# Fixing where sixteen weight tiles are converted: a data tie to a head's maxima and another order of the three integer steps

## The chip, the cores and the metric

The kernel runs on one core of a Trainium2 chip. The metric is the device time of one execution in microseconds (us). Engines are called by the names of the profile: PE (TensorE), DVE (VectorE), ACT (ScalarE), POOL (GpSimd), SP (SyncE, which only issues DMAs here).

## The reference

Block-causal attention over 8 batches of 8 heads (576 positions, head width 64), then a gated feed-forward layer over the 4608 tokens:

```python
scores = scale * np.matmul(q, k.transpose(0, 1, 3, 2))
scores = np.where(mask, scores, -1000000000.0)          # mask: block_i >= block_j, blocks of 64
scores = scores - np.max(scores, axis=-1, keepdims=True)
attn = np.exp(scores)
attn = attn / (np.sum(attn, axis=-1, keepdims=True) + 1e-09)
x = np.matmul(attn, v)                                   # then heads side by side: (4608, 512)
h = x @ w_in                                             # (4608, 2048)
sp = np.maximum(h, 0.0) + np.log1p(np.exp(-np.abs(h)))
out = (h * erf(sp)) @ w_out                              # (4608, 512)
```

The attention inputs are float32, the weights float64 (handed over as pairs of 32-bit words), the output float32.

## The kernel before, in words

**The heads.** A Python loop over n = 0 to 66 (line 663) lays out 64 heads as a software pipeline. In round n it emits the load of head n+3 (line 394: two POOL-issued DMAs into one of four buffers `qk0` to `qk3`, one SP-issued DMA into `st`), the row maxima of head n+2 (`maxes`, line 405: PE scores at L412, DVE reductions at L415 into the tile `mx0` or `mx1`, by the parity of n; L440, a PE transpose at L442, an ACT copy `mt` at L444 and a small DMA put them into the head's `qk` buffer), the probabilities of head n (`probs`: PE at L458 and L459, ACT exponentials at L463), and for every second n the product with v of the two heads before (`pv`: PE at L507 and, for the sums, L530). `normalise` (line 559) follows for each four heads: reciprocals at L570, their split into `r2` at L571 and L572 on DVE, a PE transpose `ru` at L582, scaling at L592, and the store to `x_d`.

**The weights.** 16 tiles in two halves each, so 32 conversions from float64 to float32. A conversion's 512 KB (`raw`, two buffers, line 112) is loaded by SP (L115). `to_f32` (line 118) makes a float32 from the two words of each float64: an ACT step (L122) writes `a` from the high word, and three DVE steps (L123, L124, L125) put the float32 together in `t`. L123 takes the low word alone, L124 and L125 read `a`. A last ACT step (L128) sums the squares. `a` lies in the tag `r0`, three buffers that the gate of the feed-forward layer uses too. The table `TOF` (line 641) says in which rounds conversions are emitted: one in rounds 0 and 1, two in rounds 2 to 8 and 11 to 18. In rounds 9 and 20 `scale_group` (line 545) turns the sums of squares of a group of eight tiles into a scale, and `split_w` (line 143) makes float16 pairs.

**The feed-forward layer.** From round 10 on `moe1` (line 271) puts pieces of it between the attention's (`up` at L193, `gate` at L161 to L169, `down` at L202), as far as attention has finished tokens and tiles of weights are split. What is left runs after the loop, in the code from line 714 on.

**What sets the order.** `merge` (line 217) interleaves the pieces of a round by fractions of the round. This is the program's order; a scheduler then decides in what order each engine gets its instructions. It lets an instruction go ahead of earlier ones where nothing that it reads or writes holds it back, so a conversion can be put into an engine's queue ahead of the round that emitted it. Each engine works through its queue in that order and stands still when the next instruction has to wait.

The functions that the diff touches, and their callers:

Of the kernel before, what the change touches and what calls it, by code (L numbers as in the profile page):

```python
# [14 lines left out]
ALU = mybir.AluOpType  # L15
# [8 lines left out]
def f32(ap):  # L24
    return ap.bitcast(F32)


def i32(ap):
    return ap.bitcast(I32)
# [3 lines left out]
def tile_attention_moe(ctx: ExitStack, tc: tile.TileContext, qk, v, w, maskrows, selws, out):  # L33
    nc = tc.nc
# [66 lines left out]
    def raw_t(f):  # L101
        return f32(slots[f + 1].rearrange("p a b -> p (a b)"))
# [12 lines left out]
        nc.sync.dma_start(raw, w[f, s].bitcast(I32))  # L115
        return raw.rearrange("p (n t) -> p n t", t=2)

    def to_f32(f, s, raw):

        t = i32(raw_t(f)[:, s * DM : (s + 1) * DM])  # L120
        a = mpool.tile([P, DM], F32, tag="r0", name=f"a{f}_{s}")
        nc.scalar.activation(a, f32(raw[:, :, 1]), AF.Copy, scale=2.0**-112)  # L122
        nc.vector.tensor_scalar(out=t, in0=raw[:, :, 0], scalar1=29, scalar2=None, op0=ALU.logical_shift_right)  # L123
        nc.vector.scalar_tensor_tensor(out=t, in0=i32(a), scalar=3, in1=t, op0=ALU.logical_shift_left, op1=ALU.bitwise_or)  # L124
        nc.vector.scalar_tensor_tensor(out=t, in0=i32(a), scalar=-0x80000000, in1=t, op0=ALU.bitwise_and, op1=ALU.bitwise_or)  # L125
        g = group[f]
        j = f - GROUPS[g][0]
        nc.scalar.activation(a, f32(t), AF.Square, accum_out=wss[g][:, s, j : j + 1])  # L128
# [169 lines left out]
    with tc.tile_pool(name="apool", bufs=2) as apool, tc.tile_pool(name="spool", bufs=1) as spool, \  # L298
# [6 lines left out]
        mxs = [spool.tile([P, 7], F32, name=f"mx{i}") for i in range(2)]  # L305
# [83 lines left out]
        def load_qk(n):  # L389
            b, h = divmod(n, H)  # L390
            t = qks[n % NB][:, : 4 * S].rearrange("p (i n) -> p i n", n=S)
            st = apool.tile([P, S], F32, tag="st", name=f"st_{n}", bufs=2)

            def a():
                nc.gpsimd.dma_start(t[:D, 1:4, :], qk[b, h, D:].rearrange("(s d) n -> d s n", d=D))
                nc.sync.dma_start(st, qk[b, h, : 2 * D])
                nc.gpsimd.dma_start(t[D:, 0:2, :], qk[b, h, : 2 * D].rearrange("(s d) n -> d s n", d=D))

            def c():
                nc.gpsimd.tensor_tensor(out=t[:D, 0, :], in0=st[:D, :], in1=f32(t[:D, 2, :]), op=ALU.subtract)  # L400
                nc.gpsimd.tensor_tensor(out=t[D:, 1, :], in0=st[D:, :], in1=f32(t[D:, 1, :]), op=ALU.subtract)  # L401

            return a, c
# [147 lines left out]
        def scale_b(b):  # L551
            vsb = vs[b * NQ + NQ - 1][0]
            nc.vector.tensor_copy(binv[b], vsb[:, 1:2])
            for g in range(2):
                if scaled[g]:
                    scale_bg(b, g)
            known.append(b)
# [57 lines left out]
        raws = {}  # L615

        def next_raw(src=None):
            if len(raws) < len(HALVES):
                fs = HALVES[len(raws)]
                raws[fs] = load_raw(*fs, apool, src)  # L620
# [9 lines left out]
        def late(kind, steps):  # L630

            def run(f):
                tc.cur_priority += PRIO.get(kind, 0)
                f()
                tc.cur_priority -= PRIO.get(kind, 0)
            return [lambda f=f: run(f) for f in steps]
# [4 lines left out]
        TOF = {0: 1, 1: 1, 2: 2, 3: 2, 4: 2, 5: 2, 6: 2, 7: 2, 8: 2} | {n: 2 for n in range(11, 19)}  # L641
        SCALE_AT = {9: 0, 20: 1}
        SPLIT = {9: 2, 10: 3, 11: 3, 20: 2, 21: 2, 22: 2, 23: 2}
        def conv():
            fs = HALVES[len(conved)]
            conved.append(fs)
            if len(raws) < len(conved):
                next_raw()
            to_f32(*fs, raws[fs])
            if len(raws) == len(conved):  # L650
                next_raw()

# [10 lines left out]
        for n in range(N + 3):  # L663
            lists = []
            if n + NB - 1 < N:
                load, low = load_qk(n + NB - 1)
                lists += [(late("load", [load]), 0, LQ), (late("low", [low]), LQ, 1)]
            if n + 2 < N:
                *steps, rows[n + 2] = maxes(n + 2)
                lists.append((late("max", steps), 0, 1))  # L670
            if n + 1 in rows:
                lists.append((late("max", [rows.pop(n + 1)]), 0, 0.6))
            if n < N:
                prs[n] = []
                lists.append((late("prob", probs(n, prs[n])), 0, 1))
            qd = n // 4 + 1
            if n < 2:
                lists.append(([lambda v0=v32: scale_v(0, 0, *v0), lambda v0=v32: vs.__setitem__(0, prep_v(0, 0, *v0))][n : n + 1], 0.6, 0.8))
            if n % 4 == 1 and qd < N // 4:
                v32 = load_v(*divmod(qd, NQ), mxs[(n + 1) % 2][:1, 3:4])  # L680
            if n % 4 == 2 and qd < N // 4:
                lists.append((late("v", [lambda qd=qd: scale_v(*divmod(qd, NQ), *v32)]), 0, 1))
            if n % 4 == 3 and qd < N // 4:
                lists.append((late("v", [lambda qd=qd: vs.__setitem__(qd, prep_v(*divmod(qd, NQ), *v32))]), 0, 1))
            if n % 2 == 0 and 2 <= n <= N:
                j = n // 2 - 1
                qd, pp = divmod(j, 2)
                usbs[j] = apool.tile([P, S], F32, tag="usb", name=f"usb{j}", bufs=2)
                steps = pv(qd, pp, [prs.pop(2 * j), prs.pop(2 * j + 1)], vs[qd], usbs[j], rss[j % 2])
                lists.append((late("pv", steps), 0, 1))  # L690
                if pp == 1:
                    normals[n + 1] = qd
            if n in normals:
                qd = normals.pop(n)
                b, q_ = divmod(qd, NQ)
                lists.append((late("norm", normalise(b, q_, [usbs.pop(2 * qd), usbs.pop(2 * qd + 1)], rss)), 0.2, 0.8))
                if q_ == NQ - 1:
                    lists.append((late("norm", [lambda b=b: scale_b(b)]), 0, 0.2))
                    ready_at[n + 1] = (b + 1) * S // T
            ready = ready_at.get(n, ready)  # L700
            for _ in range(TOF.get(n, 0)):
                lists.append((late("conv", [conv]), 0, 1))
            if n == 2:
                lists.append(([selects], 0.5, 0.6))
            if n in SCALE_AT:
                lists.append(([lambda n=n: scale_group(SCALE_AT[n])], 0, 0.1))
            if n in SPLIT:
                lists.append((late("conv", [split_next] * SPLIT[n]), 0.1, 1))
            if n < 2:
                lists.append(([warm] * WARM, 0, 1))  # L710
            lists.append((late("moe", [lambda: moe1(ready)] * RATE[0 if n < 10 else 1 if n < 20 else 2]), 0, 1))
            merge(*lists)
# [49 lines left out]
```

## Time and profile before

| | |
|---|---|
| time, median of 3 runs | 1243.53 us (1240.6 to 1246.77) |
| the profiled execution's own time | 1237.53 us |
| its span in the profile | 1235.7 us |
| PE busy (matmuls) | 1147.4 us, 93% of the span |
| DVE busy | 811.4 us, 66% |
| ACT busy | 850.0 us, 69% |
| POOL busy | 479.1 us, 39% |
| read from and written to HBM | 121.69 MB and 28.31 MB |

The shares are means over a span whose parts differ. PE is close to full from about 300 us on. The conversions all lie in the first 240 us, where PE has idle time and where its granted clock is below full at times; so the numbers of the stretch count, not those of the span. The profiled execution took 6.0 us less than the median of the runs.

### The profile page before, as it was taken

Reading aid. Unit: us, or ns where it says so; the run is one execution under the profiler, and the core shown is the slowest. Engines: PE = TensorE matmul, PEld = TensorE weight load, DVE = VectorE, ACT = ScalarE, POOL = GpSimd, SP = SyncE. Lnnn points to the kernel's source line nnn. Section 1 sums busy time; section 2 is a strip of 40 time slices with the busy share of each in tenths; the row PEclk is TensorE's granted clock in tenths of the full one; section 3 lists DMA queues with packets and bytes.
Section 4 is the critical chain, followed back from the end, with each engine's and each line's share of the span. In section 5 each row is a group of like instructions: output and inputs, shape, how many; then the busy total and the mean of one; then the engine's idle time right before and its main releaser. Section 6 shows DMA issues by size and latency. Waiting matters only on the chain.

```text
span 1235.7 us, 23041 instructions
## 1 busy us (share of the span) xinstructions
PE 1147.4 (93%) x8874; PEld 794.2 (64%) x8874; DVE 811.4 (66%) x1535; ACT 850.0 (69%) x1651; POOL 479.1 (39%) x459
## 2 busy tenths in 40 slices
PE   6787988899999999999999999999989999999997
PEld 3454655566676667767676676776766766666663
DVE  4677797787567767677668666666667644554554
ACT  2465767587677767777777676677767776766664
POOL 6454455436443444535453444435444312100000
PEclk9787899999999999999999999999999999999999
DMA  9987667644545445444454444444444221221202
GB/s 234 246 214 191 164 186 184 189 114 121 119 130 135 113 108 136 131 134 111 115 138 101 121 117 126 110 124 114 120 114 114 57 64 56 68 68 52 69 27 77
DMA packets 95628, 151.73 MB, mean 123 GB/s; under 512 B 7611, under 2 KB 44795, under 8 KB 95519
## 3 DMA queue, kind: packets, MB, share of 16 engines
q1 hardware_dynamic: 69696, 93.34, 24.8%
q0 software_dynamic: 25152, 56.69, 21.6%
q8 instruction: 70, 1.15, 0.4%
q10 hardware_dynamic: 670, 0.23, 0.1%
q14 instruction: 40, 0.32, 0.1%
HBM read 121.69 MB, written 28.31 MB: 121 GB/s over the span
## 4 chain that ended last, share of the span: by engine, by line
PE 37%; ACT 25%; DVE 24%; DMA 7%; issue 5%; POOL 1%; ACTq 0%; DVEq 0%; SPq 0%; POOLq 0%
PE m_h L193 11%; PE o L202 11%; DVE m_r L165 6%; DVE m_r L166 5%; PE u L507 5%; DVE m_r L167 5%; ACT m_r L162 4%; ACT m_r L161 4%; ACT m_r L164 4%; ACT m_r L163 4%; DMA raw<-w 3%; ACT m_gh L168 2%; PE s L412 2%; PE t L458 2%; PE t L459 2%
## 5 line engine op out<-in xcount | busy, mean ns | idle before, releaser
L193 PE MATMUL m_h<-xh,w 128*128 128x256 f16 x2304 | 470.8, 274 | 14.5 <-DVE m_r L167 14.1
L193 PEld LDWEIGHTS <-w 128*128 128x128 f16 x3456 | 326.3, 98 | 146.7 <-issue 19.3
L202 PE MATMUL o<-w,m_gh 128*128 128x512 f16 x1152 | 334.2, 382 | 6.2 <-ACT m_gh L168 5.2
L193 PE MATMUL m_h<-xl,w 128*128 128x256 f16 x1152 | 314.9, 273 | 0.0
L415 DVE TENSOR_REDUCE mx<-s 64x1 f32<-64x288 f32 (+4 forms) x384 | 174.1, 468 | 108.7 <-PE s L412 107.9
L169 POOL TENSOR_TENSOR m_gl<-m_r,m_gh 128x512 f16<-128x512 f32 x114 | 136.6, 1199 | 272.5 <-ACT m_gh L168 244.9
L165 DVE SCALAR_TENSOR_TENSOR m_r<-m_r,m_r 128x512 f32<-128x512 f32 x144 | 116.6, 809 | 167.3 <-ACT m_r L164 161.9
L168 ACT CAST m_gh<-m_r 128x512 f16<-128x512 f32 x144 | 88.8, 617 | 176.6 <-DVE m_r L167 175.3
L202 PE MATMUL o<-w,m_gl 128*128 128x512 f16 x576 | 204.2, 385 | 0.0
L463 ACT ACTIVATE p<-t 128x288 f32<-128x288 f32 (+4 forms) x384 | 144.6, 384 | 74.4 <-PE t L459 64.1
L412 PE MATMUL s<-qk 68*64 68x288 f32 (+3 forms) x384 | 149.0, 421 | 28.7 <-DMA qk<-qk 22.2
L458 PE MATMUL t<-qk 69*128 69x288 f32 (+4 forms) x384 | 168.0, 438 | 7.4 <-DMA qk<-mt 3.7
L161 ACT ACTIVATE m_r<-m_h,c,bs 128x512 f32<-128x512 f32 (+3 forms) x192 | 124.1, 666 | 26.1 <-PE m_h L193 23.4
L202 PEld LDWEIGHTS <-m_gh 128*128 128x128 f16 x1152 | 100.7, 98 | 63.0 <-issue 8.5
L400 POOL TENSOR_TENSOR qk<-st,qk 64x576 fp32r<-64x576 f32 x64 | 94.7, 1479 | 116.1 <-DMA qk<-qk 112.6
L475 DVE TENSOR_TENSOR p<-p,p 128x832 f16<-128x832 f32 x80 | 81.5, 1018 | 63.6 <-ACT p L474 63.4
L459 PE MATMUL t<-qk 128*128 128x288 f32 (+4 forms) x384 | 120.5, 314 | 0.0
L166 DVE SCALAR_TENSOR_TENSOR m_r<-m_r 128x512 f32<-128x512 f32 x144 | 116.6, 810 | 3.2
L401 POOL TENSOR_TENSOR qk<-st,qk 64x576 fp32r<-64x576 f32 x64 | 97.3, 1520 | 34.5 <-DMA qk<-qk 30.8
L163 ACT ACTIVATE m_r<-m_r,c 128x512 f32<-128x512 f32 x144 | 103.7, 720 | 2.8 <-ACT m_r L162 0.7
L162 ACT ACTIVATE m_r<-m_r,c 128x512 f32<-128x512 f32 x144 | 103.7, 720 | 2.0
L164 ACT ACTIVATE m_r<-m_r,c 128x512 f32<-128x512 f32 x144 | 103.6, 719 | 2.1 <-ACT m_r L163 0.3
(108 smaller groups left out, 1432.4 us busy)
## 6 DMA issues: line engine op xcount, KB each, us to landing
qk<-qk POOLq DMA_DIRECT2D x64, 432.0 KB, 4.8
st<-qk SPq DMA_DIRECT2D x64, 288.0 KB
qk<-qk POOLq DMA_DIRECT2D x64, 288.0 KB, 4.9
raw<-w SPq DMA_DIRECT2D x32, 512.0 KB
v<-v SPq DMA_DIRECT2D x16, 640.0 KB
x_d<-xs POOLq DMA_DIRECT2D x32, 288.0 KB, 3.2
xh<-x_d SPq DMA_DIRECT2D x36, 256.0 KB
xl<-x_d SPq DMA_DIRECT2D x36, 256.0 KB
```

The costliest lines, as they stand in the source:

```text
L161: nc.scalar.activation(r0s[:, :, lo:hi], h[:, :, lo:hi], AF.Tanh, bias=const(p1), scale=bss[b][g][:, 0:1])
L162: nc.scalar.activation(r1, r0, AF.Square, bias=const(b1), scale=a1)
L163: nc.scalar.activation(r0, r1, AF.Square, bias=const(b2), scale=a2)
L164: nc.scalar.activation(r0, r0, AF.Square, bias=const(b3), scale=a3)
L165: nc.vector.scalar_tensor_tensor(out=r0, in0=r0, scalar=c4, in1=r1, op0=ALU.add, op1=ALU.mult)
L166: nc.vector.scalar_tensor_tensor(out=r0, in0=r0, scalar=c5, in1=r0, op0=ALU.add, op1=ALU.mult)
L193: nc.tensor.matmul(h[:, k, :], lhsT=wf[:, a, sl], rhs=x[:, cc, :], start=cc == 0 and i == 0, stop=cc == NCC - 1 and i == 2)
L202: nc.tensor.matmul(o[c], lhsT=a[:, sl], rhs=wf[:, b_, :], start=u == u0 and k == 0 and not lo and b_ == 2, stop=u == u1 - 1 and k == nu - ...
L412: nc.tensor.matmul(dst[:r, :w_], lhsT=qh[:K, i * P : i * P + r], rhs=kh[:K, k0 : k0 + w_], start=True, stop=True)
L415: nc.vector.tensor_reduce(out=mx[:r, col : col + 1], in_=src, axis=AX.X, op=ALU.max, negate=True)
L458: nc.tensor.matmul(s[:kk, :w_], lhsT=kh[:K, ks], rhs=qh[:K, q0 : q0 + w_], start=True, stop=False)
L459: nc.tensor.matmul(s[:kk, :w_], lhsT=klh[:, ks], rhs=qhl[:, q0 : q0 + w_], start=False, stop=True)
```

## The change

`to_f32` gets a fourth argument, a pointer to one element of a maxima tile, and a tiny DVE copy writes this element into the first element of `a` before the ACT step. The ACT step overwrites all of `a`, so no result changes; but it must now come after the copy, and the copy after the DVE reductions that wrote the element. `conv` passes on the argument: for the first conversion of round n column 0, for the second column 3 of `mx0` or `mx1`, which in that round belong to head n+2. And the DVE steps swap roles: the first shifts `a` left by 3, the second shifts the low word right by 29 and joins it, the third adds the sign as before. So no DVE step can run ahead of the ACT step any more, and the last reader of `raw` is the second DVE step, where it was the ACT step or the first DVE step.

```diff
-    def to_f32(f, s, raw):
+    def to_f32(f, s, raw, src):
 
         t = i32(raw_t(f)[:, s * DM : (s + 1) * DM])
         a = mpool.tile([P, DM], F32, tag="r0", name=f"a{f}_{s}")
+        nc.vector.tensor_copy(a[:1, :1], src)
         nc.scalar.activation(a, f32(raw[:, :, 1]), AF.Copy, scale=2.0**-112)
-        nc.vector.tensor_scalar(out=t, in0=raw[:, :, 0], scalar1=29, scalar2=None, op0=ALU.logical_shift_right)
-        nc.vector.scalar_tensor_tensor(out=t, in0=i32(a), scalar=3, in1=t, op0=ALU.logical_shift_left, op1=ALU.bitwise_or)
+        nc.vector.tensor_scalar(out=t, in0=i32(a), scalar1=3, scalar2=None, op0=ALU.logical_shift_left)
+        nc.vector.scalar_tensor_tensor(out=t, in0=raw[:, :, 0], scalar=29, in1=t, op0=ALU.logical_shift_right, op1=ALU.bitwise_or)
         nc.vector.scalar_tensor_tensor(out=t, in0=i32(a), scalar=-0x80000000, in1=t, op0=ALU.bitwise_and, op1=ALU.bitwise_or)
...
-        def conv():
+        def conv(src):
...
-            to_f32(*fs, raws[fs])
+            to_f32(*fs, raws[fs], src)
...
-            for _ in range(TOF.get(n, 0)):
-                lists.append((late("conv", [conv]), 0, 1))
+            for i in range(TOF.get(n, 0)):
+                lists.append((late("conv", [lambda src=mxs[n % 2][:1, 3 * i : 3 * i + 1]: conv(src)]), 0, 1))
```

From line 121 on the changed kernel's lines are one higher: the ACT step is L123 there, the DVE steps L124 to L126, the copy L121 plus one, L122.

The scheduler's order changes with it. The first place is DVE's queue in round 9, where the reciprocals of the second group of heads are split into `r2` (the PE transpose `ru` waits for it). `we0` and `wsb0` are the scale of the first weight group, `vm1_1` the maxima of a v tile, `raw8_1` the load of a conversion that round 11 emits. Before:

```order
L139 TENSOR_SCALAR we0_1137<-we0_1137 128x2
L348 TENSOR_REDUCE vm1_1_1352<-v1_1_1126 128x1
L140 TENSOR_SCALAR we0_1137<-we0_1137 128x2
...
L571 CAST r2_146<-ri0_1_1163 128x3x8
L123 TENSOR_SCALAR w9_101<-raw8_1_1519 128x512
L543 TENSOR_TENSOR bs0_0_113<-bs0_0_113,wsb0_111 128x1
L572 TENSOR_TENSOR r2_146<-ri0_1_1163,r2_146 128x3x8
```

Now:

```order
L140 TENSOR_SCALAR we0_1153<-we0_1153 128x2
L416 TENSOR_REDUCE mx1_150<-s01_11_1166 128x1
L141 TENSOR_SCALAR we0_1153<-we0_1153 128x2
...
L572 CAST r2_146<-ri0_1_1179 128x3x8
L542 SCALAR_TENSOR_TENSOR bs0_0_113<-bi0_159,wsb0_111 128x1
L543 SCALAR_TENSOR_TENSOR bs0_0_113<-bi0_159,wsb0_111 128x1
L573 TENSOR_TENSOR r2_146<-ri0_1_1179,r2_146 128x3x8
```

The step on `raw8_1` is gone from in front of the last instruction on `r2`, and the reduction `vm1_1` comes one round later.

The second place is ACT's queue in round 3, with the two conversions of tile 2 (`a2_0`, `a2_1`) between the exponentials of head 3 (`p0_3`, `p1_3`) and the copy of head 4's maxima (`mt_4`). Before:

```order
L122 ACTIVATE a2_1_578<-raw2_1_576 128x512
L463 ACTIVATE p0_3_532<-t0_3_0_537 128x288
L463 ACTIVATE p0_3_532<-t0_3_288_546 128x288
L444 CAST mt_4_556<-mt4_554 5x128
L463 ACTIVATE p0_3_532<-t3_3_320_559 128x192
L445 DMA qk0_129<-mt_4_556 1x5x128
L463 ACTIVATE p0_3_532<-t4_3_320_588 64x64
L463 ACTIVATE p1_3_533<-t1_3_128_595 128x448
L463 ACTIVATE p1_3_533<-t2_3_256_602 128x320
L122 ACTIVATE a3_0_660<-raw3_0_584 128x512
```

Now:

```order
L464 ACTIVATE p0_3_536<-t4_3_320_594 64x64
L445 CAST mt_4_560<-mt4_558 5x128
L446 DMA qk0_129<-mt_4_560 1x5x128
L123 ACTIVATE a2_0_574<-raw2_0_491 128x512
L123 ACTIVATE a2_1_583<-raw2_1_581 128x512
L464 ACTIVATE p1_3_537<-t1_3_128_601 128x448
L464 ACTIVATE p1_3_537<-t2_3_256_608 128x320
L464 ACTIVATE p0_4_613<-t0_4_0_619 128x288
```

The ACT steps of tile 2 come later, right behind one another and behind `mt_4`, and that of tile 3, which stood at the end of this piece, is now in the next round.

The third place is DVE's queue in round 4, the steps of tile 3's two halves (their result is in `w4`) among head 6's maxima. Before:

```order
L123 TENSOR_SCALAR w4_96<-raw3_0_584 128x512
L123 TENSOR_SCALAR w4_96<-raw3_1_666 128x512
L124 SCALAR_TENSOR_TENSOR w4_96<-a3_0_660,w4_96 128x512
L124 SCALAR_TENSOR_TENSOR w4_96<-a3_1_668,w4_96 128x512
L415 TENSOR_REDUCE mx0_149<-s2_6_644 128x1
L125 SCALAR_TENSOR_TENSOR w4_96<-a3_0_660,w4_96 128x512
L415 TENSOR_REDUCE mx0_149<-s3_6_657 128x1
L125 SCALAR_TENSOR_TENSOR w4_96<-a3_1_668,w4_96 128x512
L415 TENSOR_REDUCE mx0_149<-s4_6_0_682 64x1
```

Now:

```order
L122 COPY a3_0_666<-mx0_149 1x1
L126 SCALAR_TENSOR_TENSOR w3_95<-a2_1_583,w3_95 128x512
L416 TENSOR_REDUCE mx0_149<-s2_6_650 128x1
L416 TENSOR_REDUCE mx0_149<-s3_6_663 128x1
L124 TENSOR_SCALAR w4_96<-a3_0_666 128x512
L122 COPY a3_1_675<-mx0_149 1x1
L416 TENSOR_REDUCE mx0_149<-s4_6_0_690 64x1
L125 SCALAR_TENSOR_TENSOR w4_96<-raw3_0_590,w4_96 128x512
L124 TENSOR_SCALAR w4_96<-a3_1_675 128x512
L126 SCALAR_TENSOR_TENSOR w4_96<-a3_0_666,w4_96 128x512
L125 SCALAR_TENSOR_TENSOR w4_96<-raw3_1_673,w4_96 128x512
```

Two of the maxima reductions go ahead of the conversion, and `raw` is read by the second of the three steps, where it was read by the first.

## Rows read from the trace of the kernel before

**Rows 1.** Busy time by stretch; per engine us (count), then granted clock, DMA share, GB/s
```profile
25.00:105.00 80.00, 62.44 (x422) 40.62 (x421) 56.78 (x132) 43.60 (x124) 37.18 (x36) 0.81 0.93 228
115.00:125.00 10.00, 9.93 (x40) 6.64 (x40) 8.79 (x15) 6.97 (x14) 8.02 (x9) 0.50 0.39 104
125.00:250.00 125.00, 112.27 (x828) 75.70 (x825) 96.00 (x191) 85.00 (x195) 58.42 (x52) 0.93 0.68 182
300.00:1236.00 936.00, 900.95 (x7194) 630.28 (x7189) 590.78 (x1061) 666.29 (x1226) 327.65 (x298) 1.00 0.38 103
```

**Rows 2.** The page's list of DMA issues: KB each, median us to landing
```profile
qk<-qk POOLq DMA_DIRECT2D x64, 432.0 KB, 4.8
st<-qk SPq DMA_DIRECT2D x64, 288.0 KB
qk<-qk POOLq DMA_DIRECT2D x64, 288.0 KB, 4.9
raw<-w SPq DMA_DIRECT2D x32, 512.0 KB
```

**Rows 3.** The copies of maxima, one a head, 25 to 110 us: ns, first and last start
```profile
L444 ACT CAST mt<-mt x10: 238/255/257, 24.9 to 108.9; 5x128 fp32r<-5x128 f32 x10
```

**Rows 4.** Who waited for whom, 20 to 250 us: total, times, longest
```profile
ACT a L122 <- DMA raw<-w: 13.2, 4, 6.6
...
PE ru L582 <- DVE r L572: 8.6, 3, 5.0
...
DVE w L123 <- DMA raw<-w: 6.6, 5, 2.0
```

**Rows 5.** The chain of waits, 0 to 300 us: the loads of raw on it
```profile
67.21 8.01 DMA raw<-w
...
104.43 9.03 DMA raw<-w
...
181.90 6.44 DMA raw<-w
...
207.89 7.59 DMA raw<-w
```

**Rows 6.** DVE in order of time, round 9: start, us, in brackets the idle time before
```profile
108.22 0.20 DVE L139 TENSOR_SCALAR we<-we 128x2 int32<-128x2 int32 x1
109.48 1.49 DVE L348 TENSOR_REDUCE vm<-v 128x1 f32<-128x1280 f32 x1 [1.06 <-DMA v<-v]
...
113.48 0.43 DVE L123 TENSOR_SCALAR w<-raw 128x512 int32<-128x512 int32 x1 [1.28 <-DMA raw<-w]
...
113.89 0.18 DVE L572 TENSOR_TENSOR r<-ri,r 128x24 fp32r<-128x24 f32 x1
```

**Rows 7.** PE in order of time: round 9, and one later piece like the third row
```profile
108.88 0.28 PE L459 MATMUL t<-qk 128*128 128x256 f32 x1
114.22 0.80 PE L582 MATMUL ru<-ident,r 128*16 128x128 f32 x3 [5.05 <-DVE r L572]
...
120.74 5.50 PE L507 MATMUL u<-p,v 128*64 128x256 f32 x28
...
205.40 3.07 PE L507 MATMUL u<-p,v 128*64 128x256 f32 x28
```

**Rows 8.** PE in order of time: the longer waits for DVE after 125 us
```profile
159.78 0.49 PE L412 MATMUL s<-qk 68*64 68x288 f32 x1 [2.23 <-DVE mx L415]
...
172.81 0.49 PE L582 MATMUL ru<-ident,r 128*16 128x128 f32 x3 [1.47 <-DVE r L572]
...
190.17 0.47 PE L458 MATMUL t<-qk 69*128 69x448 f32 x1 [1.70 <-DVE mx L415]
...
226.76 0.49 PE L582 MATMUL ru<-ident,r 128*16 128x128 f32 x3 [2.13 <-DVE r L572]
```

**Rows 9.** Durations by line, ns least/median/most, first and last start
```profile
L122 ACT ACTIVATE a<-raw x32: 648/669/737, 23.3 to 229.6; 128x512 f32<-128x512 f32 x32
L123 DVE TENSOR_SCALAR w<-raw x32: 363/417/1632, 23.5 to 235.6; 128x512 int32<-128x512 int32 x32
L124 DVE SCALAR_TENSOR_TENSOR w<-a,w x32: 627/680/2672, 25.3 to 236.5; 128x512 int32<-128x512 int32 x32
L337 DVE COPY v<-mx x16: 131/142/143, 10.7 to 895.1; 1x1 f32<-1x1 f32 x16
```

## The prediction

> **What bounds the kernel now.** I read the table of busy time by stretch first [rows 1]. From 300 us on PE has matmuls in 901 of 936 us at full clock: that part is PE's own work, the change has no instruction in it, and whatever is won or lost before is carried to the end as a shift. The conversions lie between 23 and 238 us, where PE is busy 62 of 80 us and 112 of 125 us and its mean granted clock is 0.81 and 0.93 (levels 1.2 and 2.4 GHz). So the sum is over waits of PE in those stretches.
>
> Second, the loads. Up to 105 us DMA moves 228 GB/s at a busy share of 0.93 [rows 1]. A head needs 432 + 288 + 288 KB, and the two conversions of a round 2 x 512 KB [rows 2]: 2032 KB, 2.08 MB, at 228 GB/s 9.1 us. The copies of maxima come once a head: ten from 24.9 to 108.9 us, 9.3 us apart [rows 3]. So in rounds 2 to 8 bytes set the pace, and an engine that waits less gains little there. After 125 us DMA runs at 182 GB/s, and PE with its waits for other engines sets the pace.
>
> Third, who waits for raw. ACT waits four times, 13.2 us in all, of which the longest (6.6 us) is the start-up; DVE five times, 6.6 us [rows 4]. Both queues are in order, so what stands behind waits along. The chain of waits runs through four loads of raw, of 6.4 to 9.0 us [rows 5]; the one issued at 104.43 us is that of raw8_1, which landed at 113.46 us. Its reader on DVE is the step at 113.48 us [rows 6], two instructions ahead of the last one on r2, and PE's transposes of r2 started at 114.22 us after 5.05 us of nothing [rows 7]. This is PE's longest wait in the stretch, and the conversion that caused part of it was only needed two rounds later.
>
> **The change part by part.**
>
> *Round 9.* The order shows the raw step gone from ahead of r2's last instruction, and the reduction vm1_1 moved a round on. On DVE this takes out a wait of 1.06 and a work of 1.49 us for vm1_1, and a wait of 1.28 and a work of 0.43 us for raw8_1 [rows 6], 4.26 us of the 5.47 between the end of L139 (108.42) and the start of L572 (113.89). What remains are small steps that have their inputs. L572 then starts near 109.6 us and PE goes on at about 110.0 in place of 114.22. I take -4.2 us; the ends are -5.05 (PE never waits) and 0 (another late input, such as the maxima reductions put in there).
>
> *The clock behind it.* In the stretch 115 to 125 us the granted clock was 0.50, the 1.2 GHz level, with PE busy 9.93 of 10 us [rows 1]; PE had stood still for the 5.05 us before. The 28 matmuls with v took 5.50 us there and 3.07 us at full clock later [rows 7]. If the wait shrinks to about 1 us I expect the clock to stay up for these: -2.4 us. Ends: 0 (it falls anyway) and -5.0 (the whole stretch at double speed).
>
> *After 125 us.* Four longer waits of PE for DVE add up to 7.5 us [rows 8]. In front of r2 at 172.8 us a third conversion step is replaced by the small copy, and ahead of the maxima that PE waits for at 190.2 us a step on raw12_1 is gone; ahead of the other two the order keeps as much work. So -1.47 - 1.70 = -3.2 us; ends 0 and -7.5.
>
> *The copies.* 32 copies of one element, 0.142 us each by the nearest row, the same kind of copy for v [rows 9]: 4.5 us on DVE, which is busy 71 to 77% in these stretches [rows 1]. Only those in front of something PE waits for count: I take +1.0, ends 0 and +4.5.
>
> *The swapped steps.* The first step is again one that reads one tensor, and the second again one that reads two, both 128x512: 417 and 680 ns as before [rows 9], cost 0. What differs is that the first now reads a contiguous tile and the second a strided one; no row shows that pair, and I take the ends as plus and minus 32 x 0.1 us, mostly hidden.
>
> *The release of raw.* There are two raw buffers and, in most rounds, two conversions, so each buffer turns over once a round. Before, SP could issue the next load when the ACT step (0.67 us) and the first DVE step had read it. Now it must wait for ACT, then the first DVE step and the second: at least 0.42 + 0.68 = 1.1 us later [rows 9], more where DVE has maxima in between, as the order shows for tile 3. Who waits behind: ACT's queue, with the exponentials that free PE's banks behind the conversion. Nine of 32 loads were waited for already [rows 4]. In the first 105 us bytes set the pace and I count nothing; for two of the places later I count 1.1 us each: +2.2. Ends: 0, and the second rival's price.
>
> The Trainium skill's page "DMA: Bandwidth & Descriptors", in its section "Rules for kernel authors", says to issue a DMA early, compute, and wait for its semaphore late, and this change issues each load of weights later. By that rule the term would be the second rival's price in full; by the rows it is small, since the loads before 105 us take their time from bytes and not from when they are asked for.
>
> *Sum.* -4.2 - 2.4 - 3.2 + 1.0 + 2.2 = -6.6 us. The profiled execution took 1237.53 us (span 1235.7), so it would take 1230.9; it stands 6.0 us below the median of the runs, 1243.53, so I forecast 1237 us for a median. That is 0.53% less, hardly over the 0.5% that a measurement of this kernel can tell from no change.
>
> **The rivals.**
>
> *Little is left (within 0.5%).* The gain of round 9 comes, but the rounds before give it back: rounds 2 to 8 convert half a round later, and the 16 loads that must be there by round 9 are the same. If 4 us of the 6.6 of round 9 are lost to later loads and the waits after 125 us only change their names, -2.6 + 1 = about -2: 1241.5 us. For it speaks that bytes set the pace of that stretch, so a later start of loads is time of DMA not used; against it, that the head's own loads then come sooner. Into this case goes that the change does not do what it says: a tie to maxima that are there already holds nothing back. The order speaks against that, since the ACT steps did move.
>
> *The raw buffers become the bound (slower).* The place is ACT's queue in rounds 2 to 8. A turn of the two buffers is then a load (8.0 us for the one at 67 us [rows 5]), two ACT steps of 0.67 and two pairs of DVE steps of 1.1 us [rows 9]: 11.5 us, against 9.3 us a head. In seven rounds that is +15 us. With round 9's -6.6 and the copies' +1 the sum is +9.8, or 1253 us. It decides from the point where a load takes more than 9.3 - 3.5 = 5.8 us. For it speaks that all four loads on the chain took more than that; against it, that they took so long beside each other and beside the heads' loads, and that with fewer in flight each is shorter.
>
> **How the numbers follow.** The forecast (faster by over 0.5%, though the likeliest value is close to that bound) gets 0.41: the excerpt of round 9 is plain, and its price is read from one wait. The first rival gets 0.35. The second gets 0.24: the later release is certain, its cover is not. The range takes in the larger ends of round 9, the clock and the later waits (-5.05 - 5.0 - 5 + 1 = about -14, or 1229) and the second rival (1253); about 1 in 10 is left out on each side: 1229 to 1254. The forecast's own range is 1229 to 1241. Chances: faster 0.41, within 0.5% 0.35, slower 0.24.
>
> **What would show it.** Right: PE's wait ahead of ru in round 9 is about 1 us, the granted clock there stays near 1; no DVE step of a conversion waits for a DMA; PE's waits for r2 add up to less than 8.6 us; the tenth copy of maxima stands no later than 109 us. The second rival would show as ACT waiting for raw in most rounds from 3 to 8, far over 13.2 us in all, and the tenth copy of maxima at 115 us or later. I am wrong if the shift at 300 us differs from that at the end by over 3 us (then something in the last part changed), or if the gain comes from another place than round 9.

## The result, and the profile after

The changed kernel took **1255.65 us** (median of 4 runs, 1251.7 to 1259.34), the kernel before 1242.07 (median of 4): a ratio of 1.0127, 95% interval 1.0082 to 1.0172. It is slower by 1.3%, where 0.5% faster was forecast, and lies just above the range, 1229 to 1254 us. The profiled execution took 1256.76 us (span 1255.0).

Busy time by stretch of the changed kernel, in the columns of [rows 1], with three short stretches more:

```profile
25.00:105.00 80.00, 61.51 (x410) 40.57 (x408) 55.33 (x140) 42.99 (x118) 38.76 (x36) 0.79 0.91 219
115.00:125.00 10.00, 9.69 (x47) 6.18 (x45) 7.59 (x15) 6.91 (x15) 8.92 (x8) 0.62 0.48 109
125.00:250.00 125.00, 105.29 (x758) 68.66 (x759) 100.67 (x207) 80.97 (x186) 59.79 (x53) 0.93 0.64 171
...
206.00:212.00 6.00, 6.00 (x32) 3.12 (x32) 1.74 (x5) 3.59 (x9) 2.19 (x2) 0.56 1.13 337
240.00:250.00 10.00, 4.97 (x49) 3.12 (x48) 5.28 (x21) 4.94 (x13) 5.03 (x4) 0.94 0.45 129
250.00:260.00 10.00, 6.33 (x33) 4.54 (x33) 0.69 (x1) 0.73 (x3) 2.79 (x2) 0.54 0.95 215
300.00:1236.00 936.00, 906.81 (x7239) 636.38 (x7237) 594.66 (x1065) 668.90 (x1234) 333.17 (x305) 0.99 0.39 103
```

The three short stretches in the kernel before:

```profile
206.00:212.00 6.00, 6.00 (x51) 3.83 (x48) 5.87 (x9) 4.18 (x12) 1.41 (x1) 1.00 1.14 282
240.00:250.00 10.00, 10.00 (x101) 8.27 (x101) 2.52 (x12) 6.38 (x14) 3.31 (x4) 1.00 0.95 235
250.00:260.00 10.00, 8.28 (x60) 6.08 (x59) 9.79 (x26) 7.88 (x17) 7.03 (x7) 1.00 0.53 131
```

The stretch up to 105 us is as it was. Between 240 and 260 us PE was busy 11.3 us in place of 18.3, and from 250 us on mostly at the 1.2 GHz level (0.54). The copies of maxima (`mt_n`, one a head, as in [rows 3], where mt_10 is the tenth) date this exactly. Worked out from their starts in the two traces, and from a second execution of the changed kernel (run e8 below), in us:

```
                    0 to mt_10  mt_10-16  mt_16-19  mt_19-22  mt_22 to end
before                 108.9      90.4      38.3      45.9      952.2
changed                110.9      85.4      42.4      59.5      956.7
changed, once more     112.1      83.4      41.0      56.3      954.6
```

So the changed kernel takes 5 to 7 us less behind mt_10, where the prediction put its gain, 3 to 4 us more in rounds 16 to 18, and 10 to 14 us more at heads 20 to 22. Part of the first may be the execution: two other executions with the old conversions (runs e4 and e7 below) took 85.4 and 92.6 us there. The last column shows nothing of the change: over the 19 executions profiled here it runs from 949.8 to 957.8 us whatever was edited, and the profiled execution of before stands at its low end. PE in round 9 of the changed kernel, as in [rows 7]:

```profile
111.63 0.80 PE L583 MATMUL ru<-ident,r 128*16 128x128 f32 x3 [0.32 <-DVE bs L544]
...
118.74 4.94 PE L508 MATMUL u<-p,v 128*64 128x256 f32 x28
```

**The wait at heads 20 to 22.** PE in order of time, changed kernel: the two waits of interest.

```profile
205.16 0.61 PE L459 MATMUL t<-qk 69*128 69x288 f32 x1 [2.74 <-DVE mx L416]
205.56 0.44 PE L460 MATMUL t<-qk 128*128 128x288 f32 x1
205.94 5.66 PE L508 MATMUL u<-p,v 128*64 128x256 f32 x28
...
253.47 0.59 PE L194 MATMUL m_h<-xh,w 128*128 128x256 f16 x2 [7.67 <-DMA xh<-x_d]
```

The last row is PE's longest wait: the first matmul of the feed-forward layer's tile 2 (`m2_0` in the texts below) has no x. The chain of waits of that stretch tells why:

```profile
234.84 8.28 DMA qk<-qk
...
243.19 1.14 POOL qk L401
...
245.37 1.75 POOL qk L402
...
247.13 0.33 SPq L397
...
247.63 0.38 SPq L226
...
248.06 7.22 DMA xl<-x_d
...
255.32 4.52 PE m_h L194 x23
```

Head 21's load ends late; POOL's subtraction reads it and frees one of the two `st` buffers; SP, in whose queue the load of `st_23` stands, has waited for that; and the four loads of x for tiles 2 and 3 stand behind it in the same queue. SP's queue in the kernel before, the first x load and `st_23` with its successor:

```profile
240.03 0.38 SPq L225 DMA_DIRECT2D xh<-x_d  x1
...
242.71 12.09 SPq L396 DMA_DIRECT2D st<-qk  x2
```

There the x loads came first, at 240.03 us in place of 247.63. The program's order of these transfers did not change; the scheduler, which orders SP's queue too, put `st_23` ahead.

SP's order is not the whole of these 7.6 us. The loads of x also need the second store of x, which landed at 244.41 us, against 239.89 in the kernel before, so `st_23` held them for 3.2 us (1.9 in run e8). Of the other 4.5 us, 1.7 are a later start of that store and 2.9 its longer way (7.1 us in place of 4.2), which goes with a transfer that the change moved, the last load of raw. It and the first load of head 21, in the changed kernel and then in the one before:

```profile
234.41 0.33 SPq L115 DMA_DIRECT2D raw<-w  x1
234.84 0.63 POOL L396 DMA_DIRECT2D qk<-qk  x1
```

```profile
221.04 0.33 SPq L115 DMA_DIRECT2D raw<-w  x1
235.04 0.64 POOL L395 DMA_DIRECT2D qk<-qk  x1
```

That raw load had to wait for a buffer, which the second DVE step freed at 234.33 us. In the four executions with the whole change in all tiles (the changed kernel, e1, e8, e16) head 21's load went out 0.4 us behind the last load of raw and took 7.1 to 8.3 us, and the second store of x took 6.5 to 7.1. In the 15 others raw was 3.3 us or more ahead, and they took 4.0 to 6.0 and 4.1 to 5.5 us. No run moved that load of raw alone, so this is read from the traces and not shown by an experiment.

Waits of the changed kernel from 20 to 250 us, in the columns of [rows 4]:

```profile
ACT a L123 <- DMA raw<-w: 14.2, 5, 7.2
DVE w L124 <- ACT a L123: 12.9, 11, 3.1
```

DVE waits for ACT's step, 12.9 us in all, where it had waited 6.6 us for raw; no conversion step on DVE waits for a DMA any more, as the prediction said.

### The profile page after: what moved, and what is told of

Same layout as the page of the kernel before. It is cut to its first block, busy times and chain, and to the rows that moved or that the text cites. A ratio compares the mean times of both kernels' runs of the same rounds, so it can differ in the third digit from the quotient of the medians.

```text
span 1255.0 us, 23132 instructions
## 1 busy us (share of the span) xinstructions
PE 1157.4 (92%) x8874; PEld 798.7 (64%) x8874; DVE 820.7 (65%) x1567; ACT 851.2 (68%) x1651; POOL 480.7 (38%) x459
## 4 chain that ended last, share of the span: by engine, by line
PE 42%; DVE 23%; ACT 19%; DMA 8%; issue 5%; POOL 2%; ACTq 0%; DVEq 0%; SPq 0%; POOLq 0%
PE m_h L194 15%; PE o L203 14%; DVE m_r L166 5%; DVE m_r L167 5%; PE u L508 4%; DVE m_r L168 4%; ACT m_r L162 4%; DMA qk<-qk 4%; ACT m_r L163 3%; ACT m_r L165 3%; ACT m_r L164 3%; PE s L413 2%; PE t L459 2%; PE t L460 2%; ACT m_gh L169 2%
## 5 line engine op out<-in xcount | busy, mean ns | idle before, releaser
L194 PE MATMUL m_h<-xh,w 128*128 128x256 f16 x2304 | 475.7, 276 | 20.5 <-DVE m_r L168 12.4
L170 POOL TENSOR_TENSOR m_gl<-m_r,m_gh 128x512 f16<-128x512 f32 x114 | 136.1, 1194 | 265.4 <-ACT m_gh L169 243.6
L401 POOL TENSOR_TENSOR qk<-st,qk 64x576 fp32r<-64x576 f32 x64 | 93.7, 1464 | 124.5 <-DMA qk<-qk 120.9
L167 DVE SCALAR_TENSOR_TENSOR m_r<-m_r 128x512 f32<-128x512 f32 x144 | 119.8, 832 | 3.1
L402 POOL TENSOR_TENSOR qk<-st,qk 64x576 fp32r<-64x576 f32 x64 | 100.6, 1572 | 33.9 <-DMA qk<-qk 31.1
```

The lines of the kernel that those rows point to most:

```text
L167: nc.vector.scalar_tensor_tensor(out=r0, in0=r0, scalar=c5, in1=r0, op0=ALU.add, op1=ALU.mult)
L194: nc.tensor.matmul(h[:, k, :], lhsT=wf[:, a, sl], rhs=x[:, cc, :], start=cc == 0 and i == 0, stop=cc == NCC - 1 and i == 2)
```

## The experiments

Theory S: the loss is SP's order at heads 21 to 23. Theory T, the rival: the tie, or the longer chain of each conversion, costs the time itself. The prediction's own slower rival, raw buffers that become the bound in rounds 2 to 8, fell with the trace: ACT waited for raw 14.2 us, not far over 13.2 [rows 4], and the tenth copy stood at 110.9 us, not at 115 or later. In all diffs the line numbers of the changed kernel hold.

### e1 to e4: the one load, and the two halves of the change

e1 (in the changed kernel) and e4 (in the kernel before):

```diff
-                nc.sync.dma_start(st, qk[b, h, : 2 * D])
+                (nc.gpsimd if n == 23 else nc.sync).dma_start(st, qk[b, h, : 2 * D])
```

e2 keeps the copy and takes back the order of the steps; e3 drops the copy and keeps the new order. Their diffs, e2's first:

```diff
-        nc.vector.tensor_scalar(out=t, in0=i32(a), scalar1=3, scalar2=None, op0=ALU.logical_shift_left)
-        nc.vector.scalar_tensor_tensor(out=t, in0=raw[:, :, 0], scalar=29, in1=t, op0=ALU.logical_shift_right, op1=ALU.bitwise_or)
+        nc.vector.tensor_scalar(out=t, in0=raw[:, :, 0], scalar1=29, scalar2=None, op0=ALU.logical_shift_right)
+        nc.vector.scalar_tensor_tensor(out=t, in0=i32(a), scalar=3, in1=t, op0=ALU.logical_shift_left, op1=ALU.bitwise_or)
```

```diff
-        nc.vector.tensor_copy(a[:1, :1], src)
```

e1:

> The changed kernel, with one thing other: the load of head 23's st tile is issued by POOL instead of SP, so that the four loads of x for tiles 2 and 3 no longer stand behind it in SP's queue. Theory S (the loss is SP's queue: x waits behind a load that waits for POOL): the x loads are issued at about 244.5 us instead of 247.6, as soon as the second store of x has landed; PE's wait of 7.7 us at the first matmul of m2_0 shrinks by 3 to 7 us, the half-clock stretch of 10 us behind it goes in part, and the time is 1242 to 1249 us. Theory T (the tie and the longer chain of each conversion cost the time themselves, and the queue only shows it): no more than 3 us come back, 1252 to 1256 us.

Measured: **1240.64 us**, 1.0011 of before (0.9989 to 1.0032), a little under theory S's range. The x loads went out at 240.12 us, and PE's wait for x was 0.81 us in place of 7.67. Rows of SP's queue in e1:

```profile
232.13 0.82 SPq L248 DMA_DIRECT2D part_d<-ob  x1
240.12 0.38 SPq L226 DMA_DIRECT2D xh<-x_d  x1
```

One load on another queue takes back nearly all of 1.3%. Up to that load every engine's order in the trace is that of the changed kernel; behind it the scheduler orders the other queues anew too. mt_19 to mt_22 took 48.8 us in place of 59.5. Theory T falls as the main cause.

e2:

> The tie alone: each conversion begins with the copy of one maximum, VectorE's three steps stay in the order of before (shift of the raw word first). SP's queue has the x loads of tiles 2 and 3 ahead of head 23's st load, as before. Theory S (SP's queue): 1238 to 1246 us, PE's wait at m2_0 under 3 us. Theory T (the tie itself delays the conversions): 1250 to 1257 us, with the wait at m2_0 or another in its place.

Measured: 1245.93 us, 1.0038 (1.0015 to 1.0061). Inside theory S's range at its upper end, and PE did not wait at m2_0. What it lost lies elsewhere: no gain behind mt_10 (90.4 us), since the step on raw8_1 stays ahead of r2 and PE waited 3.15 us.

e3:

> The other half alone: VectorE's steps all behind ScalarE's step, no tie. SP's queue has the x loads of tiles 2 and 3 behind head 23's st load, as in the changed kernel. Theory S (SP's queue): 1249 to 1258 us, with a wait of 5 to 9 us at the first matmul of m2_0. Theory T (the tie costs): 1238 to 1246 us. A third theory, that the swapped steps themselves cost time at each conversion (a longer chain ScalarE to VectorE, 16 times): slower too, but with the heads late from rounds 2 to 8 on, the tenth copy of maxima at 115 us or later instead of 108.9.

Measured: 1247.69 us, 1.0068 (1.0044 to 1.0092). A miss for both: no wait at m2_0, since `st_23` could go at 242.08 us. The third theory falls too, with mt_10 at 109.95 us. It gained behind mt_10 (83.8 us) and lost in rounds 16 to 18 (44.5 us against 38.3). So SP's order is not the only place, and it costs much only where POOL is late as well.

e4:

> The control: the kernel before with head 23's st load issued by POOL. Its x loads stood ahead of that load already. Theory S: no change, 1240 to 1246 us. If moving this one load to POOL brings time by itself (POOL's queue, the two st buffers), it is faster here by as much as in the changed kernel with the same edit, and then that edit says nothing of SP's queue.

Measured: 1237.5 us, 0.9974 (0.995 to 0.9997), under theory S's range. The load on POOL is worth 2 to 3 us here by itself, though PE, DVE and ACT keep their order. That part of e1's recovery is not SP's order at heads 21 to 23: of 11.8 to 14.4 us (1.0106 or 1.0127 less 1.0011) some 9 to 12 remain.

### e5 to e7: is the lead kept, and does SP's order cost alone

e5 and e6 are e3 and e2 with e1's diff. e7 is the kernel before with a lower priority for the scheduler around the x loads, which puts those of tile 3 behind `st_23`:

```diff
+            tc.cur_priority += 3000
             nc.sync.dma_start(x, x_d[s, :, t * T : (t + 1) * T].rearrange("(c p) t -> p c t", p=P))
+            tc.cur_priority -= 3000
```

e5:

> The swapped steps without the tie, and head 23's st load issued by POOL instead of SP. With the swapped steps alone the heads were 5 us earlier than before up to the sixteenth copy of maxima, and lost that between 220 and 250 us, where SP held the x loads of tiles 2 and 3 behind that st load. Theory S (SP's queue took the gain): the lead stays, the x loads are issued by 240 us, and the time is 1233 to 1239 us, under before. Theory that the lead is lost in any case (the round that takes it has another cause, such as the last conversions or the store of x): 1242 to 1248 us, as with the swapped steps alone.

Measured: 1243.81 us, 1.0068 (1.0042 to 1.0095). Theory S missed, and the time is in the other theory's range. The lead behind mt_10 (82.5 us) went in rounds 16 to 18 (45.8 us), with PE waiting 3.42 us for r2 at 226.91 us. SP's order did not hold x, which went out 0.1 us after the second store of x had landed.

e6:

> The tie alone, and head 23's st load issued by POOL. With the tie alone the x loads already stood ahead of that load in SP's queue, and the heads were 2 us late behind round 9 and 6 us late by the seventeenth copy of maxima. Theory S, which puts that loss of 5 us to the heads' rounds 9 to 17 and not to SP's queue: little comes back, 1242 to 1248 us. If moving this one load brings time by itself, as the 2 us gained in the kernel before may say, 1239 to 1243 us.

Measured: 1246.9 us, 1.0091 (1.0056 to 1.0127): nothing came back against e2, as theory S had it.

e7:

> The kernel before with only SP's order moved: the x loads of tile 3 stand behind head 23's st load (those of tile 2 stay ahead of it, and a store of part_d comes before tile 3's). All conversions as before. Theory S: the loads of tile 3 wait for POOL's subtraction of head 21, which was done at 242.7 us in the kernel before, so they start 1 to 2 us late: 1240 to 1245 us, slower than before by 0 to 4 us; the loss is small because POOL is not late here. If SP's order by itself costs the 13 us, whatever POOL does: 1250 us or more.

Measured: 1243.24 us, 1.0039 (1.0013 to 1.0065), in the range of theory S. The loads of tile 3 went out at 247.75 us and PE did not wait for them. The number fits for another reason: 2.2 us of the profile's loss lie behind mt_10, before the edit changes any order. And the loads of tile 2, which m2_0 needs first, stayed ahead of `st_23`, so this run does not try the changed kernel's order. e3 does: with `st_23` ahead of all four loads and POOL in time, x was held for 1.2 us and PE did not wait for it.

### e8 to e11: by groups of weight tiles

e8 is the changed kernel again. e9 applies the change to group 0 (tiles 0 to 7) alone, e10 to group 1 alone, e11 is e9 with e1's diff. The tiles not named keep the old steps and no tie:

```diff
+        new = group[f] == 0
+        if new:
+            nc.vector.tensor_copy(a[:1, :1], src)
...
```

e8:

> The changed kernel once more, beside the three that follow on one chip, so that they are compared with it and not only with the kernel before. Theory S (the wait for x at the first matmul of m2_0, behind head 23's st load in SP's queue) expects that wait of 5 to 9 us in its profile again and 1250 to 1258 us.

Measured: 1252.5 us, 1.0106 (1.005 to 1.0162). SP and PE in e8:

```profile
243.01 0.33 SPq L397 DMA_DIRECT2D st<-qk  x1
243.51 0.38 SPq L226 DMA_DIRECT2D xh<-x_d  x1
```

```profile
242.32 0.46 PE L459 MATMUL t<-qk 69*128 69x288 f32 x1 [1.45 <-DMA qk<-mt]
...
249.15 0.59 PE L194 MATMUL m_h<-xh,w 128*128 128x256 f16 x2 [3.57 <-DMA xh<-x_d]
```

The time is in the range and the place is the same, but the wait is 3.57 us in place of 7.67, under the 5 to 9 expected: how late POOL is against the store of x differs from one execution to the next.

e9:

> The change for the conversions of group 0 alone (f under 8, rounds 0 to 8); those of group 1 (rounds 11 to 18) as before, without tie and with the old order of steps. SP's queue then has the x loads ahead of head 23's st load, as before. Theory S, widened by what the heads' times show (the changed kernel gains 3 to 5 us in round 9 and loses it again in round 17, where two tied conversions run back to back on VectorE, 5 us, and then at SP's queue, 10 us; both places lie in group 1): the gain of round 9 stays and nothing is lost, 1233 to 1239 us, 2 to 6 us under before. Rival, that the gain of round 9 is always given back (other work is late next, whatever the conversions do): 1239 to 1243 us. Theory T (the tied conversions cost by themselves): 1244 us or more.

Measured: 1241.26 us, 1.0015 (0.9987 to 1.0043), the rival's range. Nothing was lost late, and nothing was gained in round 9: tile 8, whose raw8_1 stood in the way, belongs to group 1 and kept its old step. DVE and PE in e9:

```profile
111.13 0.18 DVE L578 CAST r<-ri 128x24 fp32r<-128x24 f32 x1
113.57 0.43 DVE L130 TENSOR_SCALAR w<-raw 128x512 int32<-128x512 int32 x1 [2.27 <-DMA raw<-w]
...
115.26 0.17 DVE L579 TENSOR_TENSOR r<-ri,r 128x24 fp32r<-128x24 f32 x1
```

```profile
115.58 0.80 PE L589 MATMUL ru<-ident,r 128*16 128x128 f32 x3 [5.04 <-DVE bs L550]
```

This is the wait of [rows 6, 7] once more, and about half of its cause stands in one row: DVE waits 2.27 us for raw ahead of r2.

e10:

> The other half: group 0 as before, the change for the conversions of group 1 alone. SP's queue has the x loads behind two stores of part_d but ahead of head 23's st load. Theory S, widened as in the run beside it: the loss of round 17 is there (two conversions back to back on VectorE, PE waiting some 3 us for mx and half clock behind it), the one at SP's queue in part, and no gain in round 9: 1244 to 1252 us. Rival, that the loss is made by group 0's late release of the raw buffers: 1238 to 1242 us.

Measured: 1244.04 us, 1.0034 (1.0006 to 1.0063), at the low edge of theory S. It gained behind mt_10 (84.7 us), which was not expected, and lost in rounds 16 to 18 (44.4 us; PE waited 2.59 us for mx at 207.1).

e11:

> As the run with the change for group 0 alone, and head 23's st load issued by POOL, which gave the kernel before 2 us. Theory S: 1231 to 1237 us, the fastest of all; if that load was worth nothing, as the run without it.

Measured: 1240.8 us, 1.0021 (0.9992 to 1.005): as e9, and a miss for theory S.

### e12 to e14: tile by tile

The condition of e9's diff is now `f < 11` (e12), `f < 12` (e13) and `f == 8` with e1's diff (e14).

e12:

> The change for weight tiles 0 to 10 alone (rounds 0 to 13); tiles 11 to 15 as before. VectorE's order in round 9 is that of the changed kernel (no step on raw8_1 ahead of r2), SP's order at heads 21 to 23 that of before (x loads ahead of head 23's st load). Theory S, with both losses in the last conversions: the gain of round 9 stays (the eleventh copy of maxima 2 to 4 us sooner than before), nothing is lost at 196 to 212 or at 240 to 260 us, 1233 to 1239 us. Rival, that the heads give the gain back wherever it is made: 1239 to 1244 us.

Measured: **1237.08 us**, 0.9979 (0.9946 to 1.0011), in theory S's range but not clear of the kernel before. The gain behind mt_10 was kept (84.8 us), and rounds 16 to 18 took 36.7 us. In its profile heads 19 and 20 stand 6.4 us ahead of before.

e13:

> As the run beside it, with one tile more (tile 11, round 14) converted the new way. That one conversion moves SP's order: two stores of part_d and head 23's st load now come ahead of the x loads of tiles 2 and 3. The conversions of rounds 16 to 18 are those of before, so that VectorE's pair of round 17 is not there. Theory S (SP's order is the larger cost, by itself): 1243 to 1251 us, 6 to 12 us over the run beside it, the difference made between the eighteenth and the twenty-second copy of maxima. Rival, that the loss is VectorE's pair of round 17 and what follows from it: as the run beside it, within 3 us.

Measured: 1244.91 us, 1.0044 (1.0015 to 1.0072): the number fits, the mechanism was only half foreseen. One more converted tile turns SP's order and also VectorE's in round 17, although the conversions there are the old ones. DVE in e13:

```profile
197.79 2.93 DVE L131 SCALAR_TENSOR_TENSOR w<-a,w 128x512 int32<-128x512 int32 x2
200.64 2.49 DVE L132 SCALAR_TENSOR_TENSOR w<-a,w 128x512 int32<-128x512 int32 x2
203.06 0.97 DVE L422 TENSOR_REDUCE mx<-s 64x1 f32<-64x288 f32 x3
```

Four steps of two conversions stand ahead of the maxima that PE waits for (2.15 us at 203.55), and rounds 16 to 18 took 41.8 us. PE waited for x as well:

```profile
249.76 0.37 PE L200 MATMUL m_h<-xl,w 128*128 128x256 f16 x1 [4.37 <-DMA xl<-x_d]
```

e14:

> The change for the two conversions of tile 8 alone, which is enough to take the step on raw8_1 from ahead of r2 in round 9, and head 23's st load issued by POOL. All else as before. If round 9's wait for raw8_1 is worth what its trace showed (5 us of PE, and what the clock loses behind it), 1231 to 1236 us, under the kernel before with the same load moved (1237.5, 2 us under before). If that wait is not in most runs of the kernel before, or its time is filled otherwise, 1236 to 1239 us.

Measured: 1237.2 us, 0.9975 (0.9943 to 1.0006), as e4 and in the second range. With only the step on raw8_1 gone the wait changed its name:

```profile
113.94 0.80 PE L589 MATMUL ru<-ident,r 128*16 128x128 f32 x3 [3.90 <-ACT w L155]
```

### e15 to e17: SP's queue cleared, conversions left alone

On e13, the changed kernel and e12: e1's diff, and the two stores of tile 1 into `part_d` (the layer's sums over the first weight group), which stood ahead of the x loads too, issued by ACT:

```diff
-        nc.sync.dma_start((out if g else part_d)[r0 : r0 + P, :], ob)
+        (nc.scalar if g == 0 and t == 1 else nc.sync).dma_start((out if g else part_d)[r0 : r0 + P, :], ob)
```

e15:

> As the kernel with tiles 0 to 11 converted the new way, with the three transfers that stood ahead of the x loads of tiles 2 and 3 in SP's queue issued elsewhere: the two stores of part_d of tile 1 by ACT, head 23's st load by POOL. VectorE's order in round 17 stays. Theory S (SP's order): the x loads go out as soon as the second store of x has landed, PE's wait of 4.4 us for x is gone, 1237 to 1241 us, 4 to 8 us under the kernel with SP's order as it was; what is left over the kernel with tiles 0 to 10 is round 17. Rival (the loss is round 17's, or the store of x itself is late): 1242 to 1247 us.

Measured: 1244.89 us, 1.0034 (1.0012 to 1.0056), the rival's range. In e13 x went out 1.8 us after the second store of x had landed, here 0.15 us after it, and PE's wait of 4.37 us is gone as theory S had it; yet the time is as in e13 (1.0034 and 1.0044). So little of what e13 lost against e12 is SP's order: 5.1 us lie between mt_16 and mt_19, where VectorE's pair is, and 3.1 us between mt_19 and mt_22, for which no single cause was found.

e16:

> The changed kernel with the same three transfers issued by ACT and POOL. Theory S: as with head 23's st load alone moved (1240.6 us), 1236 to 1241 us, some 12 us under the changed kernel. Rival as in the run beside it: 1248 us or more.

Measured: 1243.11 us, 1.0038 (1.0008 to 1.0069). Two microseconds over theory S's range, five under the rival's; mt_19 to mt_22 in 48.0 us. In the changed kernel, SP's order is the larger part.

e17:

> The kernel with tiles 0 to 10 converted the new way, with the same three transfers moved. Its x loads were first in SP's queue already. Theory S: no more than what moving them gave the kernel before (2 us): 1234 to 1238 us. If these transfers bring time by another way, 1233 us or less.

Measured: 1238.32 us, 1.0 (0.997 to 1.003), 0.3 us over theory S's range: clearing a queue that holds nothing up gains nothing.

### How the loss divides

In the changed kernel mt_19 to mt_22 took 59.5 and 56.3 us; with SP's queue cleared 48.8 and 48.0 (e1, e16); in the kernel before 45.9. So in the changed kernel, where POOL is late, SP's order costs 7.5 to 11.5 us, 9 to 12 by the medians above. Where x was not behind `st_23` (e6 against e2, e11 against e9, e17 against e12) or POOL was in time (e5 against e3), moving it brought nothing; e4 is the exception. mt_16 to mt_19 took 36.2 to 38.3 us in the eight executions whose tiles from 11 on were converted as before, 40.3 to 45.8 us in the eleven others: converting these tiles the new way, by either half of the change, costs 2 to 10 us there. That VectorE's order is the reason is read from the traces; no run put that order back by itself. In the changed kernel, DVE then POOL in round 17:

```profile
199.24 1.79 DVE L125 SCALAR_TENSOR_TENSOR w<-raw,w 128x512 int32<-128x512 int32 x1
200.96 1.38 DVE L124 TENSOR_SCALAR w<-a 128x512 int32<-128x512 int32 x1
202.25 1.88 DVE L126 SCALAR_TENSOR_TENSOR w<-a,w 128x512 int32<-128x512 int32 x1
204.06 0.68 DVE L125 SCALAR_TENSOR_TENSOR w<-raw,w 128x512 int32<-128x512 int32 x1
204.66 0.44 DVE L416 TENSOR_REDUCE mx<-s 64x1 f32<-64x288 f32 x1
```

```profile
198.81 1.67 POOL L401 TENSOR_TENSOR qk<-st,qk 64x576 fp32r<-64x576 f32 x1 [4.70 <-DMA qk<-qk]
200.45 1.60 POOL L170 TENSOR_TENSOR m_gl<-m_r,m_gh 128x512 f16<-128x512 f32 x1
202.13 1.46 POOL L402 TENSOR_TENSOR qk<-st,qk 64x576 fp32r<-64x576 f32 x1
```

The maxima at 204.66 us end PE's wait of 2.74 us; PE's granted clock was 0.56 from 206 to 212 us (1.00 before), and the 28 matmuls with v took 5.66 us, against 3.07 [rows 7].

## Why the prediction was wrong

**The step that failed** is the sum's limit to the queues that hold conversions. It followed ACT's and DVE's order and asked of SP only when it may issue the next raw; the order of the other loads in SP's queue, which the scheduler had turned at heads 21 to 23, had no term. The larger loss, 10 to 14 us from mt_19 to mt_22 in the profiles, came from there: e1 and e16 moved `st_23` out of the way of x and took most of it back. It was that large where POOL was late as well (in e3, with POOL in time, PE did not wait for x), and there, by the traces, a second term fell short, the release of raw. The terms, one by one:

- *Release of raw*: +2.2 us was forecast, twice 1.1 us after 105 us. The trace has the last load of raw 13.4 us later than before (234.41 against 221.04), where it went out together with head 21's load, whose 8.28 us made POOL late. The sum priced a later release by DVE's steps alone, and not by what the load then runs beside.
- *Copies*: +1.0 us was forecast. They took 0.133 us each; what they cost does not stand out. mt_10 came at 110.9 and 112.1 us in place of 108.9, but at 112.1 in e4 and 111.8 in e7 too, which have none.
- *Round 9*: -4.2 us was forecast. From mt_10 to ru's transposes PE took 0.7 us in place of 5.3, and its wait ahead of ru was 0.32 us, so the reading was right for this execution. But it was less safe than it seemed: before, e4 and e7 have one order of all queues up to there, and PE waited 5.05, 2.49 and 7.04 us, as raw8_1 landed sooner or later. And e14, which moved that step alone, gained nothing over e4.
- *The clock behind it*: -2.4 us was forecast, and that was wrong. The granted clock still fell (0.62 from 115 to 125 us, 0.50 in [rows 1]), and the 28 matmuls with v took 4.94 us, against 5.50 before and the 3.07 counted on [rows 7].
- *After 125 us*: -3.2 us was forecast from two of four waits. Rounds 16 to 18 lost 4.1 and 2.7 us. "Ahead of the other two the order keeps as much work" looked at waits of before; the new wait, for mx at 205.16 us, was in none of them.
- *Swapped steps*: 0 was right for a step by itself; see the last section for what POOL adds.
- *The slower rival* had nearly the size (1253) by luck: its place, ACT's queue in rounds 2 to 8, was wrong, and its rows spoke against it. Its idea, that a later release of raw costs, comes back at heads 20 and 21.
- *The Trainium skill's page "DMA: Bandwidth & Descriptors"*, section "Rules for kernel authors", with its rule to issue loads early: the rows of SP agree with the direction, though what PE waited for in the end was x (issued at 247.63 us against 240.03), not raw.

The sign written down as a test, a shift at 300 us unlike that at the end by over 3 us, did come (14.8 at mt_23, 19.3 at the end), but for the reason under the first table. What stays open: how much head 21's load would take with the last load of raw elsewhere and all else kept, and which single instruction turns the scheduler between e12 and e13. No version beat the kernel before by a measurable half per cent; e4, e12 and e14 came nearest, at 0.9974 to 0.9979.

## What to carry to other kernels

When a scheduler orders the queues, an edit to one engine's work is an edit to all: list the moves on every queue, SP's first, and ask of each load what now stands ahead of it and what that waits for. A load that waits for a buffer should not share an in-order queue with loads that PE is about to need. Where a buffer is freed later, look at what the next load into it will run beside. A gain read from one wait of one execution is worth what the next releaser leaves of it, and that can be tried alone.

## What the runs showed of the hardware

A DVE step that started while POOL was in a `tensor_tensor` ended a fixed time after POOL's instruction: 0.55 us for the steps with two inputs (L125, L126), 0.28 us for L124, which has one. The rows of round 17 above show it. POOL's L401 runs to 200.48 us and L125 to 201.03, POOL's L170 to 202.05 and L124 to 202.34, POOL's L402 to 203.59 and L126 to 204.13. In the changed kernel 14 of the 15 two-input steps that started within such an instruction ended 0.54 to 0.59 us after it, and all ten of L124 0.28 to 0.38 us after it. Of the nine two-input steps that POOL met only after they had started, eight took 0.67 to 0.69 us, as did all 40 with no POOL arithmetic beside them; the ninth took 2.38. So these steps are not slowed by a factor: a step that comes second ends a fixed time after POOL's instruction.

This is why the pair of round 17 took some 6.5 us and not 3.6, twice 0.43 + 0.68 + 0.68, and why the three steps cost 74.3 us of DVE in all where they had cost 71.4. The Trainium skill's page "SBUF — State Buffer", section "Who interferes with whom", says that a DVE instruction with two SBUF inputs contends with a GpSimd instruction that reads SBUF; the rows agree. The same page lets one-input instructions go free outside certain modes; L124 did wait, and whether it was in such a mode no run here shows.
